# A gated delta rule with a soft mixture of experts: three of six inversions in 16-token blocks, and the second layer and the output by halves of the columns

## The chip, the core and the metric

The kernel runs on one core of a Trainium2 chip. A core has TensorE (matrix products and transposes through the matrix array, into PSUM), VectorE (DVE in the profile), ScalarE (ACT), GpSimd (POOL) and SyncE (SP, which here only issues transfers), and 16 DMA engines between HBM and the on-chip memory SBUF. Each engine works through its own queue strictly in order and waits there for what it needs. The metric is the device time of one execution in microseconds; the median of three runs of the kernel before is 316.62 us (315.55 to 317.04).

## The reference

Everything is float32. Four batches of eight heads run a delta rule over 768 tokens with head dimension 48; its output, 3072 rows of 384, goes through eight experts that see only 4 weighted mixtures ("slots") of all rows each.

```python
k_n = k / (norm(k) + 1e-6)
for t in range(S):                       # per batch and head, state 48 x 48
    y[t]  = q[t] @ state
    state = state + beta[t] * outer(k_n[t], v[t] - k_n[t] @ state)
x = y as (B * S, H * D)
logits = x @ phi                         # 3072 x 32
d = softmax of logits over rows;  slot_input = d.T @ x
h = relu(slot_input[e] @ w1[e]);  slot_out = h @ w2[e]     # w1 384 x 1024, w2 1024 x 384
out = (softmax of logits over the 32 slots) @ slot_out
```

## The kernel before

**Delta rule.** The 768 tokens are cut into 12 chunks of 64 (index n), two chunks making a group g = 0 to 5. Inside a chunk the sequential rule becomes linear algebra: with the Gram matrix of the keys, the lower triangular system (I + beta * strictly lower part) has to be inverted for each of 32 heads. A chunk's 64 tokens are two 32-token halves; both halves of 2 chunks and 32 heads give 32 x 32 matrices that VectorE inverts for a whole group at once, in `invert(g)`: `spread` (L383, a block transpose that brings the matrices into rows, one matrix per lane and slot), a few small steps for norms and beta, `scale` (L410, or L407 in a split group), then the column loop `col` (L420 and L425: one product and one subtraction for each of 31 columns, growing and shrinking in size), and `backT` (L447, the block transpose back). `join` then multiplies the two halves of a chunk together on TensorE (`j`, L495), and writes two widened, masked copies of the inverse (`tw`, on ScalarE and POOL, L484).

In a group that is in `SPLIT`, only group 0 before, the 32 x 32 matrices are inverted as two 16 x 16 blocks (`col2`, L434 and L439, 15 columns at twice the width), a second transpose `backD` brings back the diagonal blocks, and `couple(n)` joins the 16-token blocks by two products on TensorE (`z` and `v`, both in `mul`, L469: 64 small matmuls of 32 x 32 with 16 moving columns, each in two passes), an eviction on ScalarE between them (`evZ`) and a merge on VectorE (`mrg`, L473).

`step(n)` carries the state over chunk n: `ks` (L559, K times state), `r` (L561 on VectorE, R = V minus that), `tr` (L571, inverse times R, together with the chunk before's `au`, L515), `fix` (L588), `s` (L602, the new state) and `qs` (L621), with evictions on ScalarE between all of them (most of them in the helper `copy`, L178). Before that `get(g)` transposes keys and queries of the group (`trk`, `trq`, L327), forms the Gram matrices (`gram`, L346) and masks them (`mskA`, L365), and `scale_v` scales V (`vs`; for groups above 0 as 16 instructions on POOL, L531). After it the rows are transposed (`try`, L642) and routed (`lg` L656, `sl` L686 and smaller ones).

**Experts.** The 24 tiles of w1 (512 KB, L776) and 32 of w2 (384 KB, L817) are loaded into buffers of the delta rule as these come free. The first layer (`fst`, L828) runs in two sets of four experts and two halves of the columns, its result is transposed (`trh`, L846), and the second layer (`snd`, L862) accumulates all eight blocks into one PSUM bank, 384 columns wide. Then `evs` (L871), `sum` (L873), `so` (L874) make the slots' outputs, `om` (L888) multiplies them by the row softmax, 96 rows at a time on four row groups, `evo` (L893) evicts, and 16 stores of 288 KB (`st`, L902; ten on SP, six on POOL) write rows of 3072 bytes.

**Order.** Nothing is scheduled at run time: each operation is written as a small function with its reads and writes, and `ORDER`, a string of numbers, gives the order in which they are issued. Each engine gets its own operations in that order. `BANKS` gives the PSUM bank of each result and `GATES` the operation behind which each weight load is held. The order around the change, by names: VectorE `backT1 r2.0 mskA5.0 mskA5.1 spread2 ... r2.1 ... col2 x12 r3.0 ... r4.0 ... backT2 r4.1 spread3`; the loads of V wait on SP for their buffer, three of them in turn; R has two buffers.

## Time and profile before

| what | value |
|---|---|
| median of three runs | 316.62 us |
| the profiled execution's own time | 319.18 us |
| its span, first to last instruction | 317.5 us |
| mean granted TensorE clock | 0.901 |
| busy: PE, DVE, ACT, POOL | 245.4, 215.0, 174.0, 100.1 us |
| moved through DMA | 45.08 MB |

The profiled execution is 2.56 us longer than the median; the span lies 1.7 us below its own time. Busy time is a sum over stages that differ: keys, queries and values arrive in rows of 192 bytes, VectorE's inversions end with the last `backT` at 235.2 us, the first layer begins at 266.9 us and the first store is issued at 297.3 us. A busy TensorE is not one at its peak, since a matmul's record includes its way through the array. Where a row shows [.. <- ..], the engine sat idle for that long before the instruction, and the name behind the arrow is what ended the wait.

### The profile page before, as it was taken

What the parts mean: (1) busy time and instruction counts of PE and PEld (TensorE: products, weight loads), DVE (VectorE), ACT (ScalarE), POOL (GpSimd) and SP (SyncE); (2) the same over time, 40 slices, a digit from 0 to 9 for tenths busy, and PEclk for the clock granted to TensorE, in tenths of its full rate; (3) what the DMA queues carried; (4) which work ended last, traced back from release to release, by engine and by line L of the source; (5) the groups of instructions that cost most, each with busy time, mean ns of one, the idle gap of its engine ahead of it and who ended that gap; (6) DMA issues with size and microseconds to landing.
All of it is one profiled execution on the core that took longest, in us unless ns stands there. A gap on an engine that the chain in (4) does not pass through costs nothing.

```text
span 317.5 us, 13695 instructions
## 1 busy us (share of the span) xinstructions
PE 245.4 (77%) x5910; PEld 187.7 (59%) x5910; DVE 215.0 (68%) x584; ACT 174.0 (55%) x420; POOL 100.1 (32%) x215
## 2 busy tenths in 40 slices
PE   0768458879798887889759897787878988998930
...
DVE  3378899996498989888899988848793306011630
...
GB/s 103 138 111 131 112 129 6 62 124 74 55 100 95 35 100 79 8 51 78 170 89 5 96 145 142 239 204 202 196 372 177 217 281 378 323 255 2 98 306 192
DMA packets 86956, 45.08 MB, mean 142 GB/s; under 512 B 78352, under 2 KB 78480, under 8 KB 86896
## 3 DMA queue, kind: packets, MB, share of 16 engines
...
HBM read 39.47 MB, written 4.72 MB: 139 GB/s over the span
## 4 chain that ended last, share of the span: by engine, by line
PE 56%; ACT 16%; DVE 8%; issue 6%; DMA 5%; SPq 4%; POOL 1%; POOLq 0%; DVEq 0%; ACTq 0%
ACT sb L178 15%; PE pb L571 6%; PE pb L621 6%; PE pb L327 5%; PE pb L588 5%; PE pb L559 4%; PE pb L862 3%; PE pb L828 3%; PE pb L346 3%; PE pb L495 3%; PE pb L888 3%; PE pb L602 3%; PE pb L469 2%; DMA sb<-in_q_dram 2%; PE pb L515 2%
## 5 line engine op out<-in xcount | busy, mean ns | idle before, releaser
L178 ACT ACTIVATE sb<-pb 128x384 f32<-128x384 f32 (+5 forms) x252 | 113.8, 467 | 72.0 <-PE pb L588 15.5
L531 POOL TENSOR_SCALAR sb<-sb 128x48 f32<-128x48 f32 x160 | 60.7, 405 | 23.9 <-DVE sb L412 14.2
L420 DVE TENSOR_TENSOR sb<-sb 128x31 f32<-128x31 f32 (+15 forms) x155 | 53.8, 347 | 4.3
L425 DVE TENSOR_TENSOR sb<-sb 128x31 f32<-128x31 f32 (+15 forms) x155 | 53.0, 342 | 4.4
L178 ACT ACTIVATE sb<-pb,sb 128x256 f32<-128x256 f32 (+1 forms) x96 | 39.7, 450 | 21.9 <-PE pb L571 7.8
L484 POOL TENSOR_SCALAR sb<-sb 128x512 f32<-128x512 f32 x10 | 16.6, 1667 | 91.9 <-DVE sb L447 23.2
L327 PE MATMUL pb<-sb 128*128 128x128 f32 x192 | 33.1, 317 | 13.0 <-DMA sb<-in_k_dram 9.0
L327 PEld LDWEIGHTS pb<-sb 128*128 128x128 f32 x192 | 24.8, 162 | 16.7 <-issue 10.4
L346 PE MATMUL pb<-sb 48*64 48x128 f32 (+1 forms) x896 | 28.6, 269 | 6.4 <-ACT sb L178 4.9
L571 PE MATMUL pb<-sb 64*64 64x48 f32 x768 | 28.9, 228 | 4.0 <-DVE sb L365 1.6
L571 PEld LDWEIGHTS pb<-sb 64*64 64x64 f32 x768 | 26.3, 143 | 6.7 <-DVE sb L365 1.8
L346 PEld LDWEIGHTS pb<-sb 48*64 48x64 f32 x896 | 23.5, 142 | 10.4 <-ACT sb L178 7.3
L515 PE MATMUL pb<-sb 64*64 64x48 f32 x768 | 29.1, 229 | 0.6 <-issue 0.6
L621 PE MATMUL pb<-sb 128*64 128x96 f32 x352 | 22.1, 274 | 6.8 <-ACT sb L178 4.0
L588 PE MATMUL pb<-sb 64*64 64x96 f32 x384 | 22.4, 258 | 6.2 <-issue 3.5
L515 PEld LDWEIGHTS pb<-sb 64*64 64x64 f32 x768 | 26.2, 143 | 0.8 <-issue 0.7
L621 PEld LDWEIGHTS pb<-sb 128*64 128x64 f32 x352 | 17.8, 152 | 12.1 <-ACT sb L178 4.7
L902 POOL DMA_DIRECT2D out_dram<-sb x6 | 3.2, 534 | 64.5 <-DVE sb L893 62.1
L588 PEld LDWEIGHTS pb<-sb 64*64 64x64 f32 x384 | 18.2, 140 | 8.8 <-ACT sb L178 4.3
L365 DVE TENSOR_TENSOR sb<-pb,sb 128x512 f32<-128x512 f32 x24 | 16.6, 690 | 9.2 <-ACT sb L178 7.8
L559 PE MATMUL pb<-sb 128*64 128x96 f32 x352 | 19.7, 254 | 3.2 <-ACT sb L178 2.0
L561 DVE TENSOR_TENSOR sb<-sb,pb 128x384 f32<-128x384 f32 x22 | 12.1, 552 | 11.1 <-PE pb L559 7.1
...
## 6 DMA issues: line engine op xcount, KB each, us to landing
...
sb<-in_v_dram SPq DMA_DIRECT2D x24, 96.0 KB, 3.4
...
sb<-in_k_dram SPq DMA_DIRECT2D x22, 96.0 KB, 3.3
...
```

What stands on the lines that cost most here:

```text
L178: S_.activation(o, i, ACT.Copy, **kw)
L327: nc.tensor.transpose(F1(ps)[:, P * h:P * h + P], A(src)[:, x:x + P], ident())
L346: mm(A(ps)[ha(e), i, P * h:P * h + P].rearrange("p (a t) -> p a t", a=2)[:, pr[0]:pr[-1] + 1], x[hd(i), j, h, e], y[hd(i), j, h, e, pr[0]: ...
L365: V.tensor_tensor(o, x4(1), m.unsqueeze(1).unsqueeze(1).broadcast_to([P, 2, HQ, C]), op=ALU.mult)
L420: V.tensor_tensor(p(), v3(tt)[:, j:j + 1, 0:m].broadcast_to(sh), v3(lb)[:, j:j + 1, j + 1:32].rearrange("p x i -> p i x").broadcast_to(sh) ...
L425: V.tensor_tensor(t, t, p(), op=ALU.subtract)
L515: mm(F1(pY[n, j])[ha(1 - e), D * x:D * x + D], A(AA[n])[ha(e), a:a + C], A(UB[n])[ha(e), c:c + D], start=n == 0 and x == 0)
L531: G_.tensor_scalar(y, y, A(nb)[:, c:c + 1], 0.5, op0=ALU.mult, op1=ALU.mult)
L559: mm(bank(pK)[ha(e), j, 2 * D * h:2 * D * h + 2 * D], t4(n, 0)[:, j, 2 * b + h, e], bd()[:, j, b, h, e])
L571: mm(bank(pU[b])[ha(e), j, y:y + D], A(TW[g])[ha(e), a:a + C], A(R)[ha(e), c:c + D], start=x == 4 * b and j == 0)
L588: mm(bank(pU[b])[ha(e), :, y:y + D], A(BBb[g])[ha(e), a:a + C], A(U)[ha(e)].rearrange("p (j x d) -> p x j d", j=2, d=D)[:, x], start=False)
L621: mm(F1(pY[n, j])[ha(1 - e), 2 * D * h:2 * D * h + 2 * D], t4(n, 1)[:, j, h, e], bd()[:, j, h // 2, h % 2, e], start=h == 0)
```

## The change

`SPLIT` becomes groups 0, 2 and 4. The joining products get another form: their stationary operands are laid out by `gx` (from the Gram matrices) and `dx` (from the diagonal blocks, of which `backD` now transposes only a half), two masked copies each, on POOL and ScalarE; a product then needs 32 matmuls with a 48-wide stationary operand and two row halves at once, instead of 64 of 32 x 32. The widened copies are made per chunk in `widen`, and their ring has three entries of one chunk. V has two buffers instead of three, R one instead of two, the column product one instead of two.

In the experts' part the second layer is formed for one half of its columns after the other, each half with its own bank, sum, scaling, output products, evictions and stores: 12 output products of 128 rows per half, two column groups side by side in one bank, and 48 stores of 96 KB in rows of 768 bytes, 24 on SP and 24 on POOL. The right half (d = 1) comes first in the order, and the left half's second layer stands between its output products. The row softmax `cT` is kept in another layout for it (`evE`).

`ORDER`, `BANKS` and `GATES` are written anew; the diff leaves them out. In the new order VectorE runs `backT1 r2.0 mskA5.1 r2.1 spread2 ... col2 x6 r3.0 ... r3.1 ... backD2 mskA7.0 r4.0 backT2 mskA7.1 mskA6.1 spread3 ... mrg5 ... mrg4`, POOL runs `gx5.1 tw3.1 vs4 gx5.0 dx5.1 dx4.1 vs5 zeroT4 tw5.1 tw4.1`, and TensorE `ks4.0 gram6.1 gram7.1 fix3.1 z5 z4 qs3.1 v5 v4`. Also left out are a mask of two more columns (`low`), 300 more columns of SBUF, and the lists of buffers for the weights, which follow the new rings.

```diff
--- before.py
+++ after.py
 ORDER = (
...
 )
 BANKS = (
...
 )
 GATES = (
...
 )
@@ -203,16 +204,18 @@
     Yr = pl.ring(2 * HD, 4)
     YTr = pl.ring(2 * HD, 2)
     Sbd = [pl.sb(16 * 2 * D) for _ in H2]
-    Vr = pl.ring(2 * HD, 3)
-    Rr = pl.ring(2 * HD, 2)
+    Vr = pl.ring(2 * HD, 2)
+    Rr = pl.ring(2 * HD, 1)
     Ur = pl.ring(2 * HD, 2)
-    TWr = pl.ring(2048, 2)
+    TWr = pl.ring(1024, 3)
     AAr = pl.ring(1024, 5)
     KQr = pl.ring(2048, 5)
     Kr = pl.ring(16 * C, 5)
     Qr = pl.ring(16 * C, 2)
     PPr, BBr = pl.ring(1024, 2), pl.ring(1024, 3)
-    lbr, ttr, prr = pl.ring(1024, 2), pl.ring(1024, 2), pl.ring(256, 2)
+    lbr, ttr, prr = pl.ring(1024, 2), pl.ring(1024, 2), pl.ring(256, 1)
+    Gxr, Dxr = pl.ring(512, 2), pl.ring(512, 2)
+    dn, zbr = pl.sb(512), pl.ring(256, 2)
     at = lambda ring, i, size: Buf(ring[i % len(ring)], size)
     smo = [0]
 
@@ -367,10 +373,16 @@
             DVE("mskA%d.%d" % (n, j), 512, msk, r=[ps, cmA], w=[(AA[n], j)])
 
 
-    SPLIT = (0,)
-    TW = [at(TWr, g, 2048) for g in range(NG)]
+    SPLIT = (0, 2, 4)
+    TW = [at(TWr, n, 1024) for n in range(N)]
     LB = [at(lbr, g, 1024) for g in range(NG)]
     nT = [at(nTr, g, 32) for g in range(NG)]
+    GX = [at(Gxr, n, 512) for n in range(N)]
+    DX = [at(Dxr, n, 512) for n in range(N)]
+
+    def own(t, c):
+
+        return A(t).rearrange("p (x c y) -> p c x y", c=2, y=32)[:, c]
 
     def invert(g):
         lb, tt, pr = LB[g], at(ttr, g, 1024), at(prr, g, 256)
@@ -442,50 +454,67 @@
         for j in range(15 if g in SPLIT else 31):
             (col2 if g in SPLIT else col)(j)
 
-        def back(o, swap):
-            i_ = A(tt).rearrange("p (j y i) -> p i j y" if swap else "p (i j y) -> p i j y", j=2, y=16)
-            V.transpose(A(o).rearrange("p (y j i) -> p i j y", i=32, j=2), i_)
-        DVE("backT%d" % g, 1024, lambda: back(lb, 0), more=730, r=[tt], w=[lb])
         if g in SPLIT:
-            dn, zb = Buf(TWr[(g + 1) % 2], 1024), Buf(TWr[(g + 1) % 2] + 1024, 512)
-            DVE("backD%d" % g, 1024, lambda: back(dn, 1), more=730, r=[tt], w=[dn])
-            for s in H2:
-                couple(2 * g + s, dn, zb)
+            DVE("backD%d" % g, 512, lambda: V.transpose(
+                A(dn).rearrange("p (y j i) -> p i j y", i=16, j=2),
+                A(tt).rearrange("p (j y i) -> p i j y", j=2, y=16)[:, 0:16]), more=365, r=[tt], w=[dn])
+        DVE("backT%d" % g, 1024, lambda: V.transpose(
+            A(lb).rearrange("p (y j i) -> p i j y", i=32, j=2),
+            A(tt).rearrange("p (i j y) -> p i j y", j=2, y=16)), more=730, r=[tt], w=[lb])
+        for s in H2 if g in SPLIT else ():
+            couple(2 * g + s)
         for s in H2:
             join(2 * g + s)
 
-    def couple(n, dn, zb):
+    def couple(n):
         g, s = divmod(n, 2)
-        lb, pp = LB[g], PPb[g]
+        lb, pp, gx, dx, zb = LB[g], PPb[g], GX[n], DX[n], at(zbr, n, 256)
         half = lambda t: A(t)[:, 512 * s:512 * s + 512].rearrange("p (x t) -> p x t", t=32)
-        z = lambda: A(zb)[:, 256 * s:256 * s + 256].rearrange("p (x t) -> p x t", t=16)
+        half16 = lambda t: A(t)[:, 256 * s:256 * s + 256].rearrange("p (x t) -> p x t", t=16)
+        z16 = lambda: A(zb).rearrange("p (x t) -> p x t", t=16)
+        y32 = lambda t, c: own(t, c).rearrange("p x (o t) -> p x o t", t=16)
         f = lambda ps: F1(ps)[:, 0:256].rearrange("p (x t) -> p x t", t=16)
-        qd = [slice(32 * x, 32 * x + 32) for x in range(4)]
         pz, pv = pl.ps(), pl.ps()
-
-        def mul(ps, a, b):
+        for c in H2:
+            o = lambda c=c: (y32(gx, c), half(pp)[:, :, 0:16].rearrange("p (x o) t -> p x o t", o=2))
+            od = lambda c=c: (y32(dx, c), half16(dn).rearrange("p (x o) t -> p x o t", o=2))
+            POOL("gx%d.%d" % (n, c), 980, lambda o=o, c=c: G_.tensor_scalar(*o(), mk(c), None, op0=ALU.mult),
+                 r=[(pp, (s, 0)), (pp, (s, 1)), (cmk, 0)], w=[(gx, c)])
+            if c and g:
+                POOL("dx%d.%d" % (n, c), 980, lambda o=od, c=c: G_.tensor_scalar(*o(), mk(13 + c), None, op0=ALU.mult),
+                     r=[dn, (cmk, 3)], w=[(dx, c)])
+            else:
+                ACTO("dx%d.%d" % (n, c), 256, lambda o=od, c=c: copy(*o(), scale=mk(13 + c)), more=25,
+                     r=[dn, (cmk, 3)], w=[(dx, c)])
+
+        def mul(ps, a, b, k):
             for x in range(16):
-                for q in qd:
-                    mm(f(ps)[q, x], half(a)[q, x], b()[q, x], tile_position=(q.start, q.start))
-        PE("z%d" % n, 1100, lambda: mul(pz, pp, lambda: half(lb)[:, :, 16:32]), rec=256, r=[(pp, (s, 0)), (pp, (s, 1)), (lb, s)], w=[pz])
-        ACTO("evZ%d" % n, 256, lambda: copy(z(), f(pz)), r=[pz], w=[(zb, s)])
-        PE("v%d" % n, 1100, lambda: mul(pv, dn, z), rec=256, r=[dn, (zb, s)], w=[pv])
+                p0 = a.addr + 64 * (x // 2) + 16 * (x % 2)
+                for e in H2:
+                    mm(f(ps)[64 * e:64 * e + 48, x], sb[64 * e:64 * e + k, p0:p0 + 48], b()[64 * e:64 * e + k, x])
+        PE("z%d" % n, 1650, lambda: mul(pz, gx, lambda: half(lb)[:, :, 16:32], 64), rec=128, r=[gx, (lb, s)], w=[pz])
+        ACTO("evZ%d" % n, 256, lambda: copy(z16(), f(pz)), r=[pz], w=[zb])
+        PE("v%d" % n, 1650, lambda: mul(pv, dx, z16, 48), rec=128, r=[dx, zb], w=[pv])
         DVE("mrg%d" % n, 256, lambda: V.scalar_tensor_tensor(
             half(lb)[:, :, 16:32], f(pv), mk(12), half(lb)[:, :, 16:32], op0=ALU.mult, op1=ALU.add), more=55,
             r=[pv, (cmk, 3)], w=[(lb, s)])
 
-    def join(n):
+    def widen(n):
         g, s = divmod(n, 2)
-        tw, bb, lb = TW[g], BBb[g], LB[g]
+        tw, lb = TW[n], LB[g]
         for h in H2:
-            f = lambda h=h: (A(tw)[:, 1024 * s:1024 * s + 1024].rearrange("p (x c t) -> p c x t", c=2, t=32)[:, h],
+            f = lambda h=h: (A(tw).rearrange("p (x c t) -> p c x t", c=2, t=32)[:, h],
                              A(lb)[:, 512 * s:512 * s + 512].rearrange("p (x t) -> p x t", t=32))
             if g and h:
                 POOL("tw%d.%d" % (n, h), 1600, lambda f=f, h=h: G_.tensor_scalar(*f(), mk(h), None, op0=ALU.mult),
-                     r=[(lb, s), cmk], w=[(tw, (s, h))])
+                     r=[(lb, s), cmk], w=[(tw, h)])
             else:
                 ACTO("tw%d.%d" % (n, h), 512, lambda f=f, h=h: copy(*f(), scale=mk(h)), more=25,
-                     r=[(lb, s), cmk], w=[(tw, (s, h))])
+                     r=[(lb, s), cmk], w=[(tw, h)])
+
+    def join(n):
+        g, s = divmod(n, 2)
+        bb, lb = BBb[g], LB[g]
         pj = pl.ps()
 
         def ep():
@@ -565,16 +594,16 @@
                 for x in range(4 * b, 4 * b + 4):
                     for j in H2:
                         for e in H2:
-                            a = 1024 * s + P * x + C * j
+                            a = P * x + C * j
                             c = HD * j + D * x
                             y = D * (x % 4)
-                            mm(bank(pU[b])[ha(e), j, y:y + D], A(TW[g])[ha(e), a:a + C], A(R)[ha(e), c:c + D],
+                            mm(bank(pU[b])[ha(e), j, y:y + D], A(TW[n])[ha(e), a:a + C], A(R)[ha(e), c:c + D],
                                start=x == 4 * b and j == 0)
                         if n:
                             for e in H2:
                                 au_mm(n - 1, j, x, e)
             more = [(AA[n - 1], 0), (AA[n - 1], 1), (UB[n - 1], b), pY[n - 1, 0], pY[n - 1, 1]] if n else []
-            PE("tr%d.%d" % (n, b), 1100, tr, rec=128 if n else 64, r=[(TW[g], (s, 0)), (TW[g], (s, 1)), (R, b)] + more[:3],
+            PE("tr%d.%d" % (n, b), 1100, tr, rec=128 if n else 64, r=[TW[n], (R, b)] + more[:3],
                w=[pU[b]] + more[3:])
             for j in H2:
                 ACTO("evW%d.%d.%d" % (n, b, j), HD // 2, lambda b=b, j=j: copy(half(U, b)[:, j], bank(pU[b])[:, j], scale=mk(j)),
@@ -716,8 +745,8 @@
         pe2 = pl.ps()
         PE("trE%d" % m, 328, lambda: nc.tensor.transpose(F1(pe2)[:, 0:P], A(ee), ident()), rec=2, r=[ee, cident], w=[pe2])
         ACTO("evE%d" % m, P, lambda: copy(
-            A(cT).rearrange("p (x a q m) -> p m x q a", a=2, q=16, m=NG)[:, m],
-            F1(pe2)[:, 0:P].rearrange("p (x q a) -> p x q a", q=16, a=2)), r=[pe2], w=[(cT, m)])
+            A(cT).rearrange("p (e m y) -> p m e y", e=2, y=C)[:, m],
+            F1(pe2)[:, 0:P].rearrange("p (e y) -> p e y", e=2)), r=[pe2], w=[(cT, m)])
 
     def get(g):
         for n in (2 * g, 2 * g + 1):
@@ -742,6 +771,8 @@
             get(got)
             got += 1
         load_kv(v, n, VB[n], D, "v")
+        for m in range(n + 2 if n else 0, min(n + 3, N)):
+            widen(m)
         step(n)
         if n:
             turn_y(n - 1)
...
@@ -853,56 +884,54 @@
             first(qq, f)
         turnh(qq)
         load_w2(qq)
-    pso = pl.ps()
-
-    def second(qq, u):
+
+    HC = Dm // 2
+    pso = [Buf(x, 1, True) for x in H2]
+    sj = [Buf(rt[1] + HC * x, HC) for x in H2]
+    so = [Buf(rt[0] + HC * x, HC) for x in H2]
+    obs = [Buf(w1b[e, kk].addr + Dm * x, Dm) for e in range(3, 7) for kk in range(NKT) for x in H2]
+
+    def second(qq, u, d):
         def prod():
             for t in (2 * u, 2 * u + 1):
                 for j in range(4):
-                    mm(F1(pso)[32 * j:32 * j + 32, 0:Dm],
+                    mm(F1(pso[d])[32 * j:32 * j + 32, 0:HC],
                        A(hTb[qq])[:, P * t + 32 * j:P * t + 32 * j + 32],
-                       A(w2b[4 * qq + j, u])[:, Dm * (t % 2):Dm * (t % 2) + Dm], start=qq == 0 and t == 0)
-        PE("snd%d.%d" % (qq, u), 1440, prod, rec=32, r=[(hTb[qq], u // 2)] + [w2b[4 * qq + j, u] for j in range(4)],
-           w=[pso])
-    for qq in H2:
-        for u in range(4):
-            second(qq, u)
-    sj, so = Buf(rt[1], Dm), Buf(rt[0], Dm)
-    ACTO("evs", Dm, lambda: S_.copy(A(sj), F1(pso)[:, 0:Dm]), r=[pso], w=[sj])
-    p4 = pl.ps()
-    PE("sum", 900, lambda: mm(F1(p4)[:, 0:Dm], A(csel), A(sj)), rec=4, r=[csel, sj], w=[p4])
-    DVE("so", Dm, lambda: V.tensor_scalar(
-        A(so), F1(p4)[:, 0:Dm], A(sS)[:, 3:4], None, op0=ALU.mult), r=[p4, (sS, 2)], w=[so])
-
-
...
+                       A(w2b[4 * qq + j, u])[:, Dm * (t % 2) + HC * d:Dm * (t % 2) + HC * d + HC], start=qq == 0 and t == 0)
+        PE("snd%d.%d.%d" % (d, qq, u), 820, prod, rec=32, r=[(hTb[qq], u // 2)] + [w2b[4 * qq + j, u] for j in range(4)],
+           w=[pso[d]])
+
+    def put(d):
+        for qq in H2:
+            for u in range(4):
+                second(qq, u, d)
+        ACTO("evs%d" % d, HC, lambda: S_.copy(A(sj[d]), F1(pso[d])[:, 0:HC]), r=[pso[d]], w=[sj[d]])
+        p4 = pl.ps()
+        PE("sum%d" % d, 560, lambda: mm(F1(p4)[:, 0:HC], A(csel), A(sj[d])), rec=4, r=[csel, sj[d]], w=[p4])
+        DVE("so%d" % d, HC, lambda: V.tensor_scalar(
+            A(so[d]), F1(p4)[:, 0:HC], A(sS)[:, 3:4], None, op0=ALU.mult), r=[p4, (sS, 2)], w=[so[d]])
+        for mp in range(NG // 2):
+            for cj in range(4):
+                c, j = divmod(cj, 2)
+                po, ob = pl.ps(), obs.pop(0)
+
+                def om(mp=mp, cj=cj, po=po):
                     r = slice(32 * cj, 32 * cj + 32)
...
+                    for e in H2:
+                        a = HD * e + P * mp
+                        mm(F1(po)[:, HC * e:HC * e + HC], A(cT)[r, a:a + P], A(so[d])[r])
+                PE("om%d.%d.%d" % (d, mp, cj), 340, om, rec=8, r=[cT, so[d]], w=[po])
+                (DVE if cj % 2 else ACTO)("evo%d.%d.%d" % (d, mp, cj), Dm, lambda po=po, ob=ob, cj=cj: (
+                    V.tensor_copy if cj % 2 else S_.copy)(A(ob), F1(po)[:, 0:Dm]), r=[po], w=[ob])
+                for e in H2:
+                    def st(c=c, j=j, e=e, mp=mp, ob=ob):
+                        b = 2 * (1 - e) + j
+                        o = out[b * S:b * S + S, HC * d:HC * d + HC].rearrange("(m c y) d -> c m y d", c=2, y=C)
+                        (G_ if e else nc.sync).dma_start(out=o[c, 2 * mp:2 * mp + 2], in_=A(ob)[:, HC * e:HC * e + HC])
+                    DMA("st%d.%d.%d.%d" % (d, mp, cj, e), 0.9, st, 290, eng="POOL" if e else "SP", r=[ob])
+    for d in H2:
+        put(d)
     pl.run(tc)
...
 
 # ---- launch: one core; inputs and outputs as the reference has them ----
 _INS = ['q', 'k', 'v', 'beta', 'moe_phi', 'moe_w1', 'moe_w2']
```

115 lines of the change are left out of this document (48 added, 67 removed).

## The prediction

> **What bounds the kernel now.** I read the slices of the span first, then stretches of it, then groups, the chain of waits, and last the timeline of the end. PE and DVE in 40 slices of 7.9 us:
>
> ```profile
> PE   0768458879798887889759897787878988998930
> DVE  3378899996498989888899988848793306011630
> ```
>
> VectorE is at 8 or 9 tenths from slice 5 to 26 and then falls away; from there TensorE is the busy one until the last slices, when both are low. Next, stretches cut at the subtraction R = V - K S (L561) of chunks 1, 2, 4, 6, 8, 10 and 11, then at the first layer (L828), at the end of the second layer, and at the end. Columns: PE, weight loads, DVE, ACT, POOL busy, granted clock, DMA share, GB/s.
>
> ```profile
> 66.99 0.55 DVE L561 TENSOR_TENSOR sb<-sb,pb 128x384 f32<-128x384 f32 x1
> ...
> 67.00:76.80 9.80, 8.08 (x223) 6.78 (x227) 8.11 (x22) 6.96 (x17) 1.45 (x3) 0.83 0.66 86
> 76.80:107.60 30.80, 26.97 (x762) 23.33 (x760) 22.74 (x57) 23.11 (x55) 15.04 (x35) 1.00 0.48 73
> 107.60:149.20 41.60, 35.45 (x998) 28.77 (x994) 36.72 (x99) 32.28 (x79) 16.10 (x35) 1.00 0.37 62
> 149.20:197.50 48.30, 38.92 (x916) 32.81 (x916) 43.31 (x117) 31.43 (x80) 17.74 (x36) 0.86 0.48 107
> 197.50:228.00 30.50, 23.91 (x640) 19.59 (x634) 21.78 (x60) 13.13 (x30) 14.12 (x34) 0.83 0.73 203
> 228.00:247.70 19.70, 16.61 (x434) 12.49 (x436) 12.38 (x41) 12.56 (x33) 3.13 (x2) 0.91 0.77 273
> 247.70:266.90 19.20, 16.68 (x382) 13.20 (x371) 7.00 (x29) 9.79 (x30) 0.00 (x0) 1.00 0.86 276
> 266.90:291.40 24.50, 24.35 (x241) 8.86 (x241) 3.96 (x9) 3.44 (x8) 0.00 (x0) 1.00 0.66 237
> 291.40:317.50 26.10, 11.34 (x66) 4.50 (x66) 8.73 (x17) 7.29 (x17) 3.20 (x6) 0.78 0.59 181
> ```
>
> No engine bounds all of it. From 149.2 to 197.5 VectorE does (43.3 of 48.3); from 76.8 to 107.6 TensorE does (27.0 of 30.8, or 88%) with VectorE at 74%; from 266.9 on TensorE alone does; and in the last 26 us neither, there the stores leave. So work taken off VectorE is worth its time only until TensorE's in-order queue is full, and that queue is at 83% (166.6 of 199.9) over the first seven stretches.
>
> **The inversions on VectorE.** The groups of the column loop, the block transposes back, the scaling and the merge:
>
> ```profile
> L420 DVE TENSOR_TENSOR sb<-sb 128x31 f32<-128x31 f32 (+15 forms) x155 | 53.8, 347 | 4.3
> L425 DVE TENSOR_TENSOR sb<-sb 128x31 f32<-128x31 f32 (+15 forms) x155 | 53.0, 342 | 4.4
> L447 DVE STREAM_TRANSPOSE sb<-sb 128x1024 f32<-128x1024 f32 x7 | 13.6, 1969 | 0.0
> L410 DVE TENSOR_TENSOR sb<-sb 128x1024 f32<-128x1024 f32 x5 | 6.2, 1232 | 0.0
> L434 DVE TENSOR_TENSOR sb<-sb 128x30 f32<-128x30 f32 (+7 forms) x15 | 3.8, 254 | 0.5
> L439 DVE TENSOR_TENSOR sb<-sb 128x30 f32<-128x30 f32 (+7 forms) x15 | 3.8, 251 | 0.3
> L473 DVE SCALAR_TENSOR_TENSOR sb<-pb,sb 128x256 f32<-128x256 f32 x2 | 1.0, 479 | 0.0
> ```
>
> A 32-column inversion costs (53.8 + 53.0) / 5 = 21.4 us, one in 16-token blocks 3.8 + 3.8 = 7.6. Each of groups 2 and 4 therefore drops 13.8 us, 32 gaps of 0.03 us (8.7 us idle over 310 instructions) = 0.9, and half the scaling = 0.6; it gains a half transpose of the diagonal blocks (1.0) and two merges (1.0). That is -13.3 each, -26.6 for both, and -1.0 in group 0, where the full transpose becomes a half one. The larger mask setup at the start (a few small instructions) lies beside the first loads.
>
> **What TensorE gets.** Pieces of the chain of waits, start, length, line and count:
>
> ```profile
> 39.86 2.22 PE pb L469 x150
> ...
> 45.58 3.30 issue
> ...
> 53.45 1.85 PE pb L571 x64
> ...
> 92.84 0.59 PE pb L327 x4
> ...
> 95.33 0.48 PE pb L642 x3
> ...
> 103.36 0.83 PE pb L588 x16
> ...
> 118.41 1.08 PE pb L346 x32
> ...
> 122.44 1.10 PE pb L495 x32
> ...
> 245.86 0.80 PE pb L656 x24
> ```
>
> A joining product now has 128 matmul records of 32x32; the new one has 32 matmuls in two passes each, 64 records, with 48-wide stationary operands and 16 moving columns in two row halves. No row shows it. At L469's pace (2.22 / 150 = 15 ns) it is 0.95 us, at L571's (64x64 operands, 48 columns, two halves, 1.85 / 64 = 29 ns) 1.85 us. It has L571's halves and L469's moving width; I take 1.3 between. There are twelve instead of four. Group 0's four become shorter, and the stretch from 39.9 to 57.5, where they are interrupted by waits for issue (3.30 the longest), loses 256 records. What decides chunk 1's subtraction there is VectorE's queue, and it has 2.4 us less ahead of it: -1.0, two masks more (+1.4), four column pairs moved behind it (-2.8). The stretch after it gets about 1 us of that back: -1.5.
>
> The written order also moves other work. I decoded both order strings and counted by stretch, with gram 1.08, j 1.10, transposes of k and q 0.59, of y 0.48, ks, qs, fix and lg 0.8, s 0.55, tr about 1.1, each new product 1.3. Chunks 2 to 4: -1 fix, -3 qs, +1 tr, +2 trk, -3 try = -2.4. Chunks 4 to 6: +2 j, +1 lg, +3 qs, +1 s, -1 tr, -2 trk, +3 trq, -1 gram, +4 try, +4 products = +11.5. Chunks 6 to 8: three products less nine other items = -1.8. Chunks 8 to 10: +5 try, one product, less small ones = +2.9. Chunks 10 to 11: -2 lg, -3 try, +1 qs = -2.3. VectorE's own changes there are -5.5, +1, -14.6, 0 and -10.6, so after the change TensorE is the larger of the two in all five.
>
> Its time: I take the 88% of the stretch at 76.8, the one TensorE already leads. (27.0-2.4)/0.88 = 28.0 against 30.8; (35.5+11.5)/0.88 = 53.4 against 41.6; (38.9-1.8)/0.88 = 42.2 against 48.3; (23.9+2.9)/0.88 = 30.5 against 30.5; (16.6-2.3)/0.88 = 16.3 against 19.7. Together 170.4 against 170.9: nothing gained. But in the last three of them the granted clock was 0.86, 0.83 and 0.91, beside 1.00 where TensorE is dense. If it is granted in full there, their busy time shrinks by at most those factors: 36.3, 25.3 and 14.8, in all 157.8, or -13.1. Between 0 and -13 I take -10, since the dense stretches (76.8, 107.6, 247.7) all show 1.00. With the 1.5 at the start, the first layer begins 11.5 us earlier, at about 255. At 93% density and full clock the five would take 149, or 22 less.
>
> **What hides the rest.** POOL gets 16 copies of 256 columns:
>
> ```profile
> L531 POOL TENSOR_SCALAR sb<-sb 128x48 f32<-128x48 f32 x160 | 60.7, 405 | 23.9 <-DVE sb L412 14.2 <-DMA sb<-in_v_dram 6.4 <-issue 2.4
> 161.73 2.34 POOL L484 TENSOR_SCALAR sb<-sb 128x512 f32<-128x512 f32 x1 [23.16 <-DVE sb L447]
> 162.65 0.56 DVE L420 TENSOR_TENSOR sb<-sb 128x31 f32<-128x31 f32 x1
> sb<-in_v_dram SPq DMA_DIRECT2D x24, 96.0 KB, 3.4
> ```
>
> By 0.405 at 48 columns and at most 2.34 at 512 one copy is 0.8 to 1.3 us, 13 to 21 us on an engine busy 16 us in each 30 to 48. They stand in its queue around the 16 scalings of V (6.5 us per chunk), and the second halves of the widening and the products wait behind them; ACT gets eight such copies and four evictions, no dearer than VectorE's 0.48 for 256 columns, with 9 us free in its fullest stretch (107.6). V has two buffers instead of three, so six issues on SP, a landing of 3.4 us and the scaling, over 10 us, start only after the subtraction two chunks before; two chunks take 28 us or more by the sums above, the last single one 16. Where a chunk takes under 6 us this would reach the path; I cost it at nothing.
>
> The Trainium skill ("SBUF — State Buffer", Who interferes with whom) says that a VectorE instruction with two SBUF inputs and a GpSimd instruction reading SBUF share a port under an exclusive lock, and the second fully blocks. The rows above show such a meeting, 0.56 us for an instruction whose form has a mean of 0.22; the next ones under the same copy took 0.21 and 0.22. By the rule VectorE could lose up to 16 copies' length; by the trace some 0.3 us each, 5 us on an engine that no longer leads.
>
> **The end.** Second layer, sum, scaling, first store, and the rates of the transfers:
>
> ```profile
> 289.83 1.47 PE pb L862 x16
> ...
> 291.91 0.93 PE pb L873 x2
> 292.86 0.63 DVE sb L874
> ```
> ```profile
> 297.30 15.78 SPq L902 DMA_DIRECT2D out_dram<-sb  x10
> ```
> ```profile
> 0.00:10.00 10.00, 1.00 (x5) 1.03 (x6) 2.94 (x22) 1.28 (x1) 9.06 (x22) 1.00 0.84 109
> 10.00:20.00 10.00, 7.61 (x207) 6.28 (x209) 5.01 (x6) 7.20 (x18) 7.07 (x14) 0.96 1.28 129
> 300.00:310.00 10.00, 4.23 (x26) 1.50 (x22) 4.11 (x9) 2.61 (x7) 1.99 (x4) 0.79 0.98 297
> L902 POOL DMA_DIRECT2D out_dram<-sb x6 | 3.2, 534 | 64.5 <-DVE sb L893 62.1 <-ACT sb L893 2.3
> ```
>
> Before, the second layer takes 128 records of 384 columns, some 10.6 of the 24.5 us, and the first store leaves 30.4 us after the first layer's start. After, one column half comes first. A record of 192 columns lies between half of 1.47/16 and all of it; L656's 128 columns at 0.80/24 = 33 ns put it at 45 ns, 16 records at 0.72 and the half at 5.8. So: 24.5 - 10.6 + 5.8 = 19.7, plus one block of the other half, sum, scaling, output product and eviction (0.7 + 0.5 + 0.4 + 0.4 + 0.5) = 22.2: the first store leaves 8.2 us earlier. The other half's 5.1 us and its output products lie beside the stores. The last weight loads land near the end of the first half's pass; I allow 0.5.
>
> Stores now move 3072 x 384 x 4 bytes = 4.72 MB in rows of 3072 bytes at 297 GB/s with the DMA engines at 0.98: 15.9 us, of 20.2 from first issue to end, so 4.3 around them. The new rows have 768 bytes. Inputs of 192-byte rows ran at 129 GB/s. Per row and 16 engines that is 24 and 165 ns; on a line between, 768 bytes take 52 ns, 235 GB/s, 20.1 us. Ends: 15.9 and 36.6. With 235: 22.2 + 0.5 + 20.1 + 4.3 = 47.1 after the first layer's start instead of 50.6, or -3.5; with 297 it would be -7.7, though then the last half's products, ready some 9 us before the end, begin to bind. I take -5, on the side of the long rows, because issue (24 stores on SP, 24 on POOL at 0.53) runs beside them.
>
> The Trainium skill ("DMA: Bandwidth & Descriptors", its opening table) gives 512 bytes as the smallest transfer for line rate. By it the stores would keep 297 GB/s and the end be 7.7 us shorter; no run here shows 768-byte rows of this kind yet.
>
> **The sum.** -1.5 - 10 - 5 = -16.5 on the profiled execution's 319.18 (span 317.5), which stands 2.6 over the median of 316.62. Against the median: 300.
>
> **Rivals.** *VectorE's relief goes through whole.* TensorE packs to 93% at full clock and the stores keep their rate: -1.5 - 22 - 7.7, 286. For it: the full granted clock follows dense work. Against: chunk steps alternate TensorE and ACT, and even 247.7 to 266.9, with VectorE nearly idle, is at 87%. *TensorE is full already.* The middle gains only the 1.5 us, the end 5: 310. For it: my sum without the clock is zero, and chunks 4 to 6 get heavier by 11.5 us. Against: 48.3 us led by VectorE at 90% lose 14.6 of its work. *Nothing arrives*, the middle as in the last case and stores at 190 GB/s (24.8 us, end +1.2): 316. *Slower: short rows.* The 768-byte stores pay as the shortest input rows do, 109 GB/s at the start: 43.3 + 4.3 + 22.2 + 0.5 = 70.3 instead of 50.6, +19.7 - 11.5, 325. It decides below 134 GB/s, where 35.1 us of transfer eat the 11.5 and the 8.2. For it: those rows are the only short ones seen, and the next slice's 129 lies under that point too. Against: 768 is four times as long, and writes go out from all partitions.
>
> **How the numbers follow.** Forecast 300 with 0.50, relief whole 0.17, TensorE full 0.17, nothing 0.07, short rows 0.09. The first three are faster: 0.84; no change is 315 to 318.2, half a percent, about what a measurement of this kernel can tell: 0.07; slower 0.09. The range holds the forecast and its two neighbours with the products' bounds (twelve at 0.95 or 1.85, 4 to 7 us either way): 286 to 313.
>
> **What would show it.** The column loop of 32 at 3 groups, some 64 us for both lines; joining products at 15 to 29 ns a record; chunks 2 to 4 shorter, 4 to 6 longer, and TensorE above VectorE in each; a granted clock nearer 1.00 from 150 on; first layer near 255; first store 22 us after it, at 200 to 300 GB/s. Wrong would be: VectorE waiting at the merges (L473's successor) for products held up by POOL's copies, TensorE waiting for the last weights, or stores bound by issue.

## The result, and the profile after

The changed kernel takes 376.91 us (median of four executions, 371.76 to 380.16) against 316.83 of the kernel before on the same chip: 1.1799 times as long, 95% interval 1.1659 to 1.1939. The forecast was 300, so it is wrong, in sign and by 77 us. The ratios in this document are made without each kernel's slowest executions (the granted clock varies from one to the next), so that they may differ by one to two per cent from the quotient of the medians.

The profiled execution took 375.93 us, its span is 373.1. The slices of the span (9.3 us each), DMA share and transfer rate:

```profile
DMA  8998816343920254453647978887973244411110
GB/s 109 136 115 121 92 25 86 69 84 65 114 47 4 43 89 89 77 111 90 151 139 223 214 241 264 315 278 219 329 267 123 51 83 85 81 47 46 47 47 31
```

In the last nine slices, where before the stores ran at 297 GB/s with the DMA engines at 0.98, the rate falls to between 51 and 85 GB/s and then to 47, and the engines' share from four tenths to one. The stretches are cut at the same events as before up to the first layer (subtraction of chunks 1, 2, 4, 6, 8, 10 and 11; chunk 8's here at its second half, 0.7 us late), then at the first store and at 318. Columns: PE, weight loads, DVE, ACT, POOL busy, granted clock, DMA share, GB/s:

```profile
68.30:80.50 12.20, 11.42 (x330) 10.28 (x332) 9.92 (x25) 6.87 (x17) 6.69 (x17) 0.86 0.37 69
80.50:107.60 27.10, 22.90 (x688) 19.46 (x688) 18.65 (x51) 21.82 (x52) 17.98 (x42) 1.00 0.61 91
107.60:159.50 51.90, 49.72 (x1299) 42.66 (x1303) 38.02 (x100) 36.31 (x90) 26.01 (x54) 0.90 0.33 59
159.50:205.20 45.70, 41.30 (x1145) 36.44 (x1137) 31.02 (x85) 30.75 (x77) 14.91 (x37) 0.89 0.54 140
205.20:231.60 26.40, 21.86 (x657) 17.56 (x657) 22.88 (x60) 14.61 (x35) 12.23 (x33) 1.00 0.85 234
231.60:245.40 13.80, 11.47 (x362) 9.65 (x364) 2.48 (x9) 9.63 (x26) 3.13 (x2) 1.00 0.87 297
245.40:266.70 21.30, 17.73 (x363) 13.82 (x358) 9.22 (x40) 9.99 (x32) 0.00 (x0) 0.92 0.81 266
266.70:289.60 22.90, 22.89 (x303) 11.03 (x303) 5.24 (x12) 4.29 (x10) 0.00 (x0) 1.00 0.60 222
289.60:318.00 28.40, 14.28 (x170) 10.35 (x166) 6.21 (x12) 5.23 (x12) 16.23 (x21) 0.77 0.37 73
318.00:373.10 55.10, 0.00 (x0) 0.00 (x0) 0.00 (x0) 0.00 (x0) 2.93 (x4) 0.50 0.18 50
```

Two things are to be read here. The first layer begins at 266.7 us, where it began in the profile before (266.9): between these two profiles the middle brought nothing. And after the first store at 289.6 the kernel runs another 83.5 us, 55 of them with TensorE, VectorE and ScalarE idle and four stores left for POOL to issue. The groups and the store's own line say what the two rest on:

```profile
L432 DVE TENSOR_TENSOR sb<-sb 128x31 f32<-128x31 f32 (+15 forms) x93 | 32.6, 351 | 2.7
L437 DVE TENSOR_TENSOR sb<-sb 128x31 f32<-128x31 f32 (+15 forms) x93 | 32.3, 347 | 2.7
L446 DVE TENSOR_TENSOR sb<-sb 128x30 f32<-128x30 f32 (+7 forms) x45 | 11.6, 258 | 1.2
L451 DVE TENSOR_TENSOR sb<-sb 128x30 f32<-128x30 f32 (+7 forms) x45 | 11.6, 257 | 1.2
L494 PE MATMUL pb<-sb 64*48 64x16 f32 (+1 forms) x768 | 26.5, 218 | 2.8 <-ACT sb L179 1.6
L494 PEld LDWEIGHTS pb<-sb 64*48 64x48 f32 (+1 forms) x768 | 25.8, 160 | 4.5 <-issue 2.9
L930 SPq DMA_DIRECT2D out_dram<-sb x24: 511/2009/12055, 289.5 to 363.3; - x24
```

VectorE's 32-column loops fell as said, from 106.8 us in five groups to 64.9 in three, and the block loops rose from 7.6 to 23.2. TensorE is busy with the twelve joining products for 26.5 us, 2.2 each. And the 24 stores on SP are issued until 363.3, one holding the queue for up to 12 us. POOL has issued its 24 by 322.4 and they land some 12 us after their issue, so that most of the last 50 us is SyncE's stores; why POOL's went faster no run asked.

### The profile page after: what moved, and what is told of

Read it like the earlier page. It is cut to its first block, busy times and chain, and to the rows that moved or that the text cites. A ratio compares the mean times of both kernels' runs of the same rounds, so it can differ in the third digit from the quotient of the medians.

```text
span 373.1 us, 14558 instructions
## 1 busy us (share of the span) xinstructions
PE 263.0 (70%) x6328; PEld 214.1 (57%) x6328; DVE 191.7 (51%) x525; ACT 177.2 (47%) x429; POOL 121.9 (33%) x249
## 4 chain that ended last, share of the span: by engine, by line
PE 48%; DVE 10%; ACT 9%; DMA 8%; issue 6%; POOL 3%; SPq 2%; POOLq 0%; DVEq 0%
ACT sb L179 9%; PE pb L494 7%; PE pb L352 5%; PE pb L333 4%; PE pb L650 4%; DMA out_dram<-sb 4%; PE pb L898 3%; PE pb L617 3%; PE pb L600 3%; PE pb L859 3%; DMA sb<-in_q_dram 3%; PE pb L588 3%; POOL sb L560 3%; PE pb L922 2%; PE pb L524 2%
## 5 line engine op out<-in xcount | busy, mean ns | idle before, releaser
L179 ACT ACTIVATE sb<-pb 48x384 f32<-48x384 f32 (+5 forms) x256 | 113.8, 463 | 60.3 <-PE pb L333 13.3
L560 POOL TENSOR_SCALAR sb<-sb 128x48 f32<-128x48 f32 x160 | 51.2, 346 | 53.0 <-PE pb L631 22.0
L179 ACT ACTIVATE sb<-pb,sb 128x256 f32<-128x256 f32 (+1 forms) x96 | 40.0, 455 | 27.1 <-PE pb L352 12.7
L333 PE MATMUL pb<-sb 128*128 128x128 f32 x192 | 33.7, 318 | 12.8 <-DMA sb<-in_k_dram 8.7
L930 POOL DMA_DIRECT2D out_dram<-sb x24 | 19.2, 801 | 68.2 <-DVE sb L924 57.9
L352 PE MATMUL pb<-sb 48*64 48x128 f32 (+1 forms) x896 | 31.4, 282 | 8.7 <-ACT sb L179 4.0
L432 DVE TENSOR_TENSOR sb<-sb 128x31 f32<-128x31 f32 (+15 forms) x93 | 32.6, 351 | 2.7
L437 DVE TENSOR_TENSOR sb<-sb 128x31 f32<-128x31 f32 (+15 forms) x93 | 32.3, 347 | 2.7
L352 PEld LDWEIGHTS pb<-sb 48*64 48x64 f32 x896 | 25.6, 150 | 12.5 <-ACT sb L179 5.7
L600 PEld LDWEIGHTS pb<-sb 64*64 64x64 f32 x768 | 25.2, 137 | 8.5 <-issue 4.9
L544 PE MATMUL pb<-sb 64*64 64x48 f32 x768 | 28.0, 223 | 2.5 <-issue 2.5
L600 PE MATMUL pb<-sb 64*64 64x48 f32 x768 | 27.8, 222 | 2.5 <-DVE sb L590 0.9
L494 PE MATMUL pb<-sb 64*48 64x16 f32 (+1 forms) x768 | 26.5, 218 | 2.8 <-ACT sb L179 1.6
L494 PEld LDWEIGHTS pb<-sb 64*48 64x48 f32 (+1 forms) x768 | 25.8, 160 | 4.5 <-issue 2.9
L544 PEld LDWEIGHTS pb<-sb 64*64 64x64 f32 x768 | 25.1, 137 | 0.3 <-issue 0.3
```

The costliest lines, as they stand in the source:

```text
L179: S_.activation(o, i, ACT.Copy, **kw)
L333: nc.tensor.transpose(F1(ps)[:, P * h:P * h + P], A(src)[:, x:x + P], ident())
L352: mm(A(ps)[ha(e), i, P * h:P * h + P].rearrange("p (a t) -> p a t", a=2)[:, pr[0]:pr[-1] + 1], x[hd(i), j, h, e], y[hd(i), j, h, e, pr[0]: ...
L432: V.tensor_tensor(p(), v3(tt)[:, j:j + 1, 0:m].broadcast_to(sh), v3(lb)[:, j:j + 1, j + 1:32].rearrange("p x i -> p i x").broadcast_to(sh) ...
L437: V.tensor_tensor(t, t, p(), op=ALU.subtract)
L494: mm(f(ps)[64 * e:64 * e + 48, x], sb[64 * e:64 * e + k, p0:p0 + 48], b()[64 * e:64 * e + k, x])
```

## The experiments

**The stores.** A store of the changed kernel writes 128 rows of 768 bytes, and its pattern in HBM runs slowest over two groups, then over 64 tokens. My theory after the result: a transfer is spread over the DMA engines by its slowest index, so each store gets 2 of 16. The rivals are that 768-byte rows are slow in themselves, as the prediction's slower case had it, and that the 48 issues are. The first run gives each group of a store a transfer of its own:

```diff
-  dma_start(out=o[c, 2 * mp:2 * mp + 2], in_=A(ob)[:, HC * e:HC * e + HC])
+  for x in H2:
+      dma_start(out=o[c, 2 * mp + x], in_=A(ob)[C * x:C * x + C, HC * e:HC * e + HC])
```

> The changed kernel with each store of 128 rows of 768 bytes split into its two token groups, so that the slowest index of each store runs over 64 rows instead of over 2 groups; twice as many stores, everything else as it is. Engines theory (a store whose slowest index has two values is given to 2 of the 16 DMA engines): the stores get all 16 and take some 15 to 25 us from their first issue at 289.6, so that the kernel ends at about 310 to 318 of its profile instead of 373. Short rows theory (768-byte rows are slow in themselves): rows are unchanged, the end stays at 365 to 377. Issue theory (the 48 stores' issues and descriptors are what is slow): 96 issues instead of 48, the end moves later, beyond 385.

It took 326.36 us (two executions), above the 310 to 318 of the engines theory and far below what the other two said: 50 of the 60 us are gone with the same rows and twice the issues. The issues then show, since POOL is busy with 48 of them for 24.8 us, but that is the smaller matter. The next run keeps 48 stores and gives each 128 consecutive tokens:

```diff
-  for e in H2:  mm(F1(po)[:, ...e], A(cT)[r, a:a + P], A(so[d])[r])       # one c, two groups m
+  for e in H2:
+      for x in H2:                                                       # both c, one group m
+          mm(F1(po)[ha(x), ...e], A(cT)[32 * (2 * x + j):..., a:a + C], A(so[d])[...])
-  out=o[c, 2 * mp:2 * mp + 2]
+  out=out[b * S + P * (2 * mp + c):b * S + P * (2 * mp + c) + P, HC * d:HC * d + HC]
```

> The changed kernel with the output products ordered so that one output tile holds 128 consecutive tokens of one batch pair; each of the 48 stores then writes 128 rows of 768 bytes whose slowest index has 128 values. Same bytes, same row length, same number of stores. Engines theory: by the 36 ns that one 768-byte packet took, 6144 packets on 16 engines are 13.8 us, so the stores keep up with the products (last one at 303.6) and the kernel takes 309 to 318 us, just under the kernel before. Short rows and issue theories: nothing that they name has changed, 365 to 377 us.

320.51 us, 1.0147 times the kernel before (1.0072 to 1.0221). The engines theory holds: 56 us are gone with neither rows nor issues changed. What is above its range can be put down to its end, which takes 52.0 us from the first layer on, against 49.3 in the run below that has half as many records in its output products. The third run tests row length alone, on the kernel before:

```diff
-  (G_ if byp else nc.sync).dma_start(out=o, in_=A(t)[0:MQ])
+  for x in range(4):
+      (G_ if byp else nc.sync).dma_start(out=o[:, :, 192 * x:192 * x + 192], in_=A(t)[0:MQ, 192 * x:192 * x + 192])
```

> The kernel before with each of its 16 stores cut into four by columns, so that its 3072-byte rows become 768-byte rows, 64 stores in all, each still with 16 values in its slowest index. Engines theory: 6144 packets at about 36 ns on 16 engines stay near 14 to 16 us; only the issues grow (24 on POOL at about 0.5 us each instead of 6), so 317 to 323 us. Short rows theory: 4.72 MB at the 47 to 55 GB/s seen in the changed kernel take some 90 us instead of 16, about 390 us.

323.87 us, 1.0257 (1.0175 to 1.0339), just above what issues alone were to cost: four times the stores, 768-byte rows, and no collapse. The fourth leaves rows and stores of the kernel before and changes only the slowest index, from 16 positions to 6 groups:

```diff
-  A(cT).rearrange("p (x a q m) -> p m x q a", a=2, q=16, m=NG)[:, m]
+  A(cT).rearrange("p (x a m q) -> p m x q a", a=2, q=16, m=NG)[:, m]
-  .rearrange("(m c u q a) d -> c u q m (a d)", ...)[c, g]
+  .rearrange("(m c u q a) d -> c u m q (a d)", ...)[c, g]
```

> The kernel before with two indices of the output tile's rows exchanged (16 positions and 6 groups become 6 groups and 16 positions): the same 16 stores, the same 3072-byte rows, but a slowest index of 6 instead of 16 values. Engines theory: 6 of 16 engines, 111 GB/s instead of 297, so 42.5 us instead of 15.9: about 343 us, or some 333 if only SyncE's ten stores are confined. Short rows and issue theories: neither rows nor issues have changed, 316 to 318 us.

333.77 us, 1.0571 (1.0493 to 1.0648), what was expected if only SyncE's ten stores are confined: POOL issues the last of its six at 301.8 us, SyncE the last of its ten at 316.0. Neither rows nor issues changed, so the 19 us are the slowest index. Rates in stretches in which little but stores runs, of the changed kernel, of this run, and of the changed kernel with a slowest index of 64 (the next run), in this order:

```profile
345.00:371.00 26.00, 0.00 (x0) 0.00 (x0) 0.00 (x0) 0.00 (x0) 0.00 (x0) 0.50 0.13 44
```
```profile
318.00:330.00 12.00, 0.00 (x0) 0.00 (x0) 0.00 (x0) 0.00 (x0) 0.00 (x0) 0.50 0.29 108
```
```profile
298.00:310.00 12.00, 6.54 (x74) 5.35 (x66) 4.06 (x8) 3.82 (x9) 9.73 (x17) 0.86 0.80 248
```

In the first two rows only SyncE's stores are left. A share of 0.13 is 2.1 of 16 engines, at 44 GB/s some 21 each; 0.29 is 4.6 engines at 108; 0.80 is 12.8 at 248. Rate by engine hardly differs (19 to 23 GB/s), the number of engines does. The Trainium skill states this rule ("DMA: Bandwidth & Descriptors", Why a DMA increments its semaphore by 16 and not by 1, and again Rules for kernel authors, Use all 16 engines): a transfer goes to the largest number up to 16 that divides the slowest dimension of both patterns. The three rows agree with it: 2.1 engines busy where it gives 2, 4.6 where it gives 6, 12.8 where it gives 16.

The smallest mending exchanges two indices of the output tile, token before group, and changes nothing else:

```diff
-  A(cT).rearrange("p (e m y) -> p m e y", e=2, y=C)[:, m]
+  A(cT).rearrange("p (e w y m) -> p w m e y", e=2, m=2, y=C)[:, m // 2, m % 2]
-  .rearrange("(m c y) d -> c m y d", c=2, y=C)        # out=o[c, 2 * mp:2 * mp + 2]
+  .rearrange("(w m c y) d -> c w y m d", c=2, m=2, y=C)   # out=o[c, mp]
```

> The changed kernel with one pair of indices exchanged in the order of the output tile's rows: a store's slowest index then runs over 64 tokens instead of 2 groups. Output products (4 records each), stores (48) and rows (768 bytes) stay as in the changed kernel. Engines theory: the stores keep up, the last output product ends some 37 us after the first layer's start as in the changed kernel, and the end follows it by 4 to 6 us: 305 to 313 us. If the kernel with consecutive tokens was slow at its end for another reason than its doubled output products (8 records each), this one takes 318 us or more.

319.19 us, 1.0141 (1.0066 to 1.0217): above its range by 6. Its end, from the first layer to the first store and from there to the end of the span:

```profile
265.80:290.20 24.40, 24.40 (x303) 11.13 (x303) 5.14 (x12) 4.21 (x10) 0.00 (x0) 0.93 0.56 205
290.20:315.10 24.90, 14.34 (x174) 10.35 (x166) 6.27 (x13) 5.30 (x12) 14.91 (x24) 0.83 0.61 191
```

That is 49.3 us where the expectation had 41 to 43: the last output product ends after 39.3 of them instead of 37, and 10 us follow it instead of 4 to 6. Against the 50.6 us of the kernel before it is short all the same. So 58 of the 60 us lost were the stores, and with them mended the change is still slower by some 4, which must lie ahead of this end. The next run puts the middle of the kernel before in front of the same end:

```diff
  # before.py, with its SPLIT = (0,), products, memory and order up to the second layer
+ # second layer, sums, output products and stores by halves of the columns, slowest index 64
```

> The middle of the kernel before (one group inverted in blocks, old products, its memory and order) with the end of the run before this one (second layer and output by halves of the columns, slowest index of 64). TensorE theory (the new products fill what VectorE gives up, the changed middle gains nothing or loses): 0 to 6 us less than the run before this one. Relief theory of the prediction (the changed middle is some 10 us shorter, and the profile of the changed kernel was an unlucky one): 8 to 12 us more than the run before this one. Against the kernel before, the end alone should give -6 to -10 us: 305 to 309.

311.65 us, 0.9928 (0.988 to 0.9976). The end by halves alone gains 3.5 us by medians (2.3 by the ratio), less than the 6 to 10 expected, and the changed middle costs 7.5 more than the old one (6.7 by the ratios). The profiles agree: the first layer begins at 260.3 us here and at 265.8 in the run with the mended stores, and what follows takes 47.8 us here and 49.3 there. The profile before, with its first layer at 266.9, was of a late execution; where the same middle was profiled again, with the cut rows and with the slowest index of 6, the first layer begins at 260.6 and 261.4. This is also the version that beats both, the kernel before by less than a per cent. A last run on its end moved six of the last stores to ScalarE's queue, as SP and POOL issue theirs without a gap from 298.8 us on, 0.54 to 0.62 us each:

```diff
-  (G_ if e else nc.sync).dma_start(...)
+  x = not d and (mp, cj, e) in ((2, 1, 0), (2, 1, 1), (0, 2, 0), (0, 1, 0), (0, 1, 1), (2, 3, 1))
+  (nc.scalar if x else G_ if e else nc.sync).dma_start(...)
```

> The best kernel so far (middle of the kernel before, end by halves with a slowest index of 64), with six of its last stores issued by ACT instead of SyncE and POOL. Issue theory of its end (both queues are busy without a gap from 298 us on, 0.54 to 0.62 us for each store, while the products end at 297.6): 1 to 3 us less, 308.5 to 310.5. If the landing of the bytes sets the end: no change, 311 to 312.

Its median is 312.57 (305.83 to 315.21), its ratio 0.9809 (0.9742 to 0.9875): the one says no change, the other 1%. Not settled.

**The middle.** Theory: the new products fill what VectorE gives up. Rival: POOL's copies and V's two buffers hold it. First the products are made cheap, everything around them kept:

```diff
-  for x in range(16):
-      p0 = a.addr + 64 * (x // 2) + 16 * (x % 2)
-      for e in H2:
-          mm(f(ps)[64 * e:64 * e + 48, x], sb[64 * e:64 * e + k, p0:p0 + 48], b()[64 * e:64 * e + k, x])
+  for e in H2:
+      mm(f(ps)[64 * e:64 * e + 48], sb[64 * e:64 * e + k, a.addr:a.addr + 48], b()[64 * e:64 * e + k])
```

> The changed kernel with the stores mended, and each of the 12 joining products computed by one 256-column matmul for each half instead of 16 of 16 columns (the product's value is left out; its operands, copies on POOL and ACT, evictions and merges stay). TensorE theory: 12 times about 1.7 us are taken off a TensorE busy 91 of 97.6 us between chunks 4 and 8: the first layer starts 10 to 18 us earlier than with the whole products. Queue theory (POOL's 20 new copies and V's two buffers hold the middle): within 3 us of the run with whole products.

305.15 us, 0.9708 (0.9581 to 0.9834), 14.0 less than with whole products. Products and the two heavy stretches (chunks 4 to 6, 6 to 8), first with whole products, then with cheap ones (there chunks 2 to 4 as well):

```profile
L494 PE MATMUL pb<-sb 64*48 64x16 f32 (+1 forms) x768 | 24.4, 210 | 3.4 <-DVE sb L461 2.9
...
105.80:157.80 52.00, 49.80 (x1299) 42.79 (x1303) 38.00 (x100) 36.26 (x90) 26.24 (x53) 0.90 0.34 59
157.80:201.50 43.70, 38.51 (x1144) 33.58 (x1136) 30.54 (x84) 30.40 (x77) 14.82 (x37) 0.96 0.54 141
```
```profile
L492 PE MATMUL pb<-sb 64*48 64x256 f32 (+1 forms) x48 | 8.4, 434 | 4.8 <-DVE sb L461 2.6 <-ACT sb L179 1.6 <-DVE sb L371 0.6
...
77.50:103.20 25.70, 23.12 (x699) 19.82 (x691) 18.19 (x52) 22.31 (x53) 17.26 (x39) 1.00 0.64 92
103.20:151.80 48.60, 43.23 (x1061) 34.70 (x1065) 37.86 (x101) 36.24 (x90) 26.75 (x56) 0.96 0.38 64
151.80:190.70 38.90, 32.95 (x904) 26.68 (x896) 30.37 (x84) 30.12 (x77) 14.97 (x37) 1.00 0.61 164
```

Of 16.0 us of TensorE taken off, 14 are missing from the median. In the profiles the first layer begins 15.0 us earlier: 8.2 of these lie in the two heavy stretches and 2.6 ahead of them; 4.2 lie behind chunk 8, where no product stands, and there the granted clock differs as well (0.89 and 1.00 between chunks 10 and 11), so that not all of the 14 need be the products. In the first heavy stretch of the changed order TensorE is the bound, busy 96% of it. The copies and V's buffers are all still in this run, so they do not hold the middle at 319. Does the relief of VectorE bring something by itself? The kernel before, with the block loop's steps alone in groups 2 and 4:

```diff
-  (col2 if g in SPLIT else col)(j)
+  (none if g in (2, 4) and j >= 15 else col2 if g in (0, 2, 4) else col)(j)
```

> The kernel before with VectorE's relief alone: groups 2 and 4 run the 15 column steps of the block form instead of 31, and nothing joins the blocks (the rest of their inversion is left out), so that VectorE has some 29 us less and TensorE, POOL and ScalarE have what they had, in the same order. Relief theory of the prediction: the stretch led by VectorE (43.3 of 48.3 us) gives back 8 to 13, in all -10 to -20 us against the kernel before. Order theory (the chunks' chain over TensorE and ScalarE sets the time whatever VectorE does): 0 to -4 us.

314.58 us, 0.9986 (0.9945 to 1.0028): nothing. The stretch that VectorE was to bound (chunks 6 to 8), with what VectorE waits for between chunks 4 and 8: the middle of the kernel before as it is (profiled in the run with the cut rows), and then relieved:

```profile
148.60:195.90 47.30, 36.93 (x939) 31.18 (x940) 43.03 (x117) 30.81 (x79) 18.00 (x35) 0.93 0.50 110
...
DVE sb L365 <- ACT sb L178: 2.6, 4, 0.8
```
```profile
152.40:200.20 47.80, 39.04 (x918) 32.97 (x918) 30.84 (x86) 31.20 (x80) 14.56 (x36) 0.86 0.49 107
...
DVE sb L365 <- ACT sb L178: 12.9, 6, 8.4
DVE sb L666 <- PE pb L659: 6.1, 1, 6.1
```

VectorE is busy 30.8 us instead of 43.0 and the stretch keeps its length. The granted clock of the two rows differs (0.93 and 0.86), but the best kernel's profile, shown further down, has the unrelieved stretch at 0.86 too, and there it takes 47.9 us. The freed time has turned into waits: VectorE comes sooner to the masks of the next Gram products (L365) and to the maximum of the routing logits (L666), whose inputs TensorE and ScalarE still deliver at their old places in the order. Now the other way round, VectorE's old work put back into the changed order with cheap products:

```diff
  # groups 2 and 4: each of the 15 block steps emits two (the last one three) of the 31 steps of the 32-column loop
```

> The run with the cheap products (one matmul for each half, values left out), in which VectorE's old work is put back: the operations of the 15 block steps of groups 2 and 4 emit the 31 steps of the 32-column loop, some 27 us of VectorE, in the changed order. If the relief counts as soon as the written order uses it, this run is 6 to 14 us above the one with cheap products: 311 to 319. If the order alone brought that run's gain, it stays within 3 us: 302 to 308.

333.30 us, 1.0523 (1.0422 to 1.0624), 28.2 more than without it (25.7 by the ratios). Chunks 2 to 4 and 6 to 8:

```profile
77.60:116.10 38.50, 27.17 (x702) 23.40 (x702) 31.35 (x84) 22.10 (x52) 16.18 (x38) 0.87 0.42 64
...
165.60:220.60 55.00, 35.75 (x904) 29.02 (x892) 43.78 (x115) 30.48 (x77) 17.69 (x37) 0.84 0.44 116
```

In these stretches VectorE has 13.2 and 13.4 us more than with the relief (18.2 and 30.4 there) and they are 12.8 and 16.1 longer. This lies outside both expectations: the same steps that were free in the old order cost all they take, and more, in the new one with its cheap products. Some of this is not the steps themselves, since the granted clock is 0.87 and 0.84 where it was 1.00 without them. I read it so that an order is written around the work it was made for.

What then sets the middle of the kernel before? First TensorE alone is relieved; a quarter of each product `j` is left:

```diff
-  for h in range(H):          # in the product j of join(n)
+  for h in range(H // 4):
```

> The kernel before with a quarter of each of its 12 products j (two heads of eight, 8 matmuls of 32; the rest is left out): TensorE has some 12 times 0.8 us less, VectorE, ScalarE, POOL and the order are as before. TensorE theory (its in-order queue sets the middle of the kernel before as well, though VectorE is busier there): 4 to 10 us less than the kernel before, 305 to 311. Relief theory of the prediction (VectorE leads from 149 to 197 us): 0 to 3 us less, 312 to 315.

314.01 us, 0.999 (0.9946 to 1.0035). On its line TensorE's time fell from 14.8 to 6.0:

```profile
L495 PE MATMUL pb<-sb 64*64 64x64 f32 x384 | 14.8, 233 | 2.5 <-DVE sb L447 2.1 <-ACT sb L178 0.3
```
```profile
L495 PE MATMUL pb<-sb 64*64 64x64 f32 x96 | 6.0, 259 | 3.7 <-DVE sb L447 3.7
```

Both reliefs at once (the last two edits together):

> The kernel before with both reliefs at once: VectorE's 27 us of column steps in groups 2 and 4 left out, and three quarters of each product j left out (TensorE). Each alone left the time where it was (ratios 0.999 and 0.999). If the two engines take turns as the bound, both together give 5 to 10 us: 305 to 310. Order theory (each engine arrives at operations whose inputs the written order makes late, in turn on TensorE, ScalarE and VectorE): 0 to -3 us: 311.5 to 315.

313.36 us, 1.0008 (0.9948 to 1.0069): nothing again, with 12.8 us of waits at L365. They do not take turns. And the chain of each chunk's steps, by its copies on ScalarE:

```diff
+  cut = D if n > 1 else 4 * D
-  copy(half(U, b)[:, j], bank(pU[b])[:, j], scale=mk(j))          # evW; evU and evS likewise
+  copy(half(U, b)[:, j, 0:cut], bank(pU[b])[:, j, 0:cut], scale=mk(j))
```

> The kernel before with ScalarE's three copies in each chunk's chain (scaled result, corrected result, state) cut to a quarter of their columns from chunk 2 on, the rest left out; VectorE, TensorE and the order as before. If the chain of chunk steps over TensorE and ScalarE sets the middle, each of 10 chunks loses about 4 copies of 0.2 us on its way: 6 to 10 us less, 305 to 309. If the order binds by late operations elsewhere (masks of the gram products, column steps of group 3): 0 to -3 us, 311.5 to 315.

309.95 us, 0.989 (0.9837 to 0.9942), 3.5 to 4.7 us less. So part of the middle is this chain, which no busy share shows, but less than the 6 to 10 of a chain that set everything. The cut also takes 18 us of work off ScalarE (174.0 us busy before, 156.0 here), so the chain and ScalarE's load are not told apart, and what sets the rest of the old middle stays open.

At last POOL's copies for the products of groups 2 and 4, cut to an eighth, with whole products:

```diff
+  u = 1 if g else 8
-  o = lambda c=c: (y32(gx, c), half(pp)...)              # dx likewise
+  o = lambda c=c: (y32(gx, c)[:, 0:u], half(pp)...[:, 0:u])
```

> The changed kernel with the stores mended (slowest index of 64), and its copies of the products' operands for groups 2 and 4 cut to an eighth of their columns (the rest of these operands is left out), on POOL and ACT alike; instructions, order and products stay. Queue theory (these copies, in POOL's queue around the scalings of V and on VectorE's port, hold the middle up): 4 to 10 us less than the run with whole copies, 309 to 315. TensorE theory: within 2 us of it, 317 to 321.

Its median, 317.25 us (310.68 to 321.87), is 1.9 under the run with whole copies; its ratio, 0.9923 (0.9854 to 0.9992), stands 2.2% under that run's 1.0141. The one says that copies cost next to nothing, the other 7 us. The profile, of its fastest execution, has 52.4 us between chunks 4 and 6 with TensorE busy 95% of them, where it was 52.0 with whole copies, so that the copies do not hold up the heaviest stretch; the stretches behind it are 0.3 to 1.8 us shorter. What they cost in all stays open, and with it the price of the shared port. V with two buffers instead of three was not tried by itself.

## Why the prediction was wrong

**Where the 60 us are.** By medians: stores on few engines +57.7 (376.91 to 319.19), changed middle +7.5 (319.19 to 311.65), end by halves -3.5 (311.65 to 315.14). The prediction had -5 for the end with its stores and -11.5 for the rest.

**The end: the transfer's step failed.** The first store was to leave 22.2 us after the first layer and left after 22.9 (24.4 in the mended kernel, at a granted clock of 0.93). The half pass, the sum and the output products were sized well. What failed is "Per row and 16 engines": the rate was worked out from the length of the rows and taken on all engines. The length was sized on the safe side, for in the mended kernel the same rows went at 248 GB/s where I had 235, and from the first store to the end it took 24.9 us where I had 24.4. But the store's pattern, given in the diff (`c m y d`, two values of m), was never compared with the pattern before, whose slowest index had 16 values. The page of the Trainium skill that I weighed, "DMA: Bandwidth & Descriptors", has the length in its opening table; the rule that decided stands further down on the same page. The "short rows" rival had the sign and not the cause: run on its own, the row length cost 8 to 9 us with its issues, and its point of decision (134 GB/s) was passed for another reason.

**VectorE's relief: right in size, wrong in worth.** It lost 23.3 us of busy time. "From 149.2 to 197.5 VectorE does" bound the kernel was false: 43.3 of 48.3 us busy, and 12.2 of them less changed nothing. Here a busy share of 90% meant that VectorE's work was spread to fill the time, not that it led. What I should have asked is what VectorE would wait for next: the masks of the Gram products.

**The products: mis-sized by the clock.** I took 1.3 us between 0.95 and 1.85; TensorE is busy with each for 2.2 in the changed kernel and 2.03 in the mended one. These sums hold a product's last record to its end. Counted from start to start, as the price was, a product takes 2.03 and 1.85. Two pairs of them in the mended kernel, 128 records each, cut at their first and last start:

```profile
108.37:111.13 2.76, 2.76 (x128) 2.76 (x125) 2.10 (x3) 2.66 (x8) 1.80 (x5) 1.00 0.02 6
113.40:118.47 5.07, 5.07 (x129) 5.07 (x128) 3.04 (x8) 0.74 (x1) 1.69 (x1) 0.50 0.01 3
```

At full clock a product takes 1.4 us (22 ns a record), as priced; at half clock 2.5 (40 ns). The clock by slices of that run (7.9 us each, counted from 0) falls longest in slices 5 to 7 and 14 to 15:

```profile
PEclk9978975699999967999999989989998978999995
```

Four of the twelve products lie wholly at half clock there, two of the four in group 0 and the pair above; (8 x 1.4 + 4 x 2.5) / 12 is 1.8, and others are hit in part. Twelve at 0.55 to 0.73 us too little are 7 to 9 us, where the range had 4 to 7 for them, and the run with cheap products shows that TensorE's time counts there. The half clock between chunks 4 and 6 goes with the whole products: all five profiles that have them show it there for some 10 us, the two with cheap products for 3.4, and those with the old products not at all or for 3.4. What in the products brings it on was not tried.

**The stretches.** Without the clock I had 28.0, 53.4, 42.2, 30.5, 16.3 us for chunks 2 to 11, in all 170.4; the changed kernel has 27.1, 51.9, 45.0, 27.1, 13.8, in all 164.9. TensorE's share came out between 82 and 96%, so 88% was fair as a mean and too low for the heaviest stretch. But the same five stretches of the old middle, 170.9 in the execution profiled, are 163.7 in the best kernel's profile, which has that middle:

```profile
77.40:108.30 30.90, 26.79 (x761) 23.16 (x758) 22.73 (x56) 23.18 (x55) 14.98 (x35) 1.00 0.48 73
108.30:149.90 41.60, 35.53 (x1001) 28.79 (x995) 36.81 (x100) 32.30 (x79) 16.12 (x35) 1.00 0.37 62
149.90:197.80 47.90, 39.03 (x917) 32.99 (x917) 43.04 (x116) 31.24 (x80) 18.11 (x36) 0.86 0.50 107
197.80:222.40 24.60, 20.16 (x637) 17.09 (x634) 21.77 (x59) 13.14 (x30) 16.26 (x34) 1.00 0.86 251
222.40:241.10 18.70, 15.14 (x436) 11.67 (x437) 12.35 (x41) 12.57 (x33) 3.14 (x2) 1.00 0.84 290
```

The low clock from 197 to 248 us (0.83, 0.91), from which I hoped to gain, changes from one execution of this code to the next: here it is 1.00 and 1.00, in the run with the cut rows 0.88 and 0.91 (the five stretches take 165.5 us there), in the one with the slowest index of 6 0.94 and 0.91 (164.8). The profile that I read was the slowest of the four. This is where "between 0 and -13 I take -10" failed: 5 to 7 us of what there seemed to be to gain lay in the execution read and not in the order. And the clock was not granted in full where TensorE became dense: 0.90 and 0.89 in the two stretches in which it is busy 96% and 90%, 0.96 and 1.00 with cheap products. The rival "TensorE is full already" described the middle best of all, and it too was on the good side: by medians the changed middle lost 7.5.

**The start and the last stretch.** -1.5 us at the start became +3.7 in the changed kernel (chunk 2's subtraction at 80.5 instead of 76.8) and +1.4 between the mended and the best kernel (78.8, 77.4). With cheap products it is 77.5, so the first products at the new price account for the mended kernel's share; in the changed kernel's profile the clock is also lower there (0.86 between chunks 1 and 2). From chunk 11 to the first layer 21.3 us took the place of 19.2, where I had no change.
